# One attention-and-MLP kernel: a new written-out order of all steps, and twelve more products of ones

## Chip, cores and metric

The kernel runs on one core of one Trainium2 chip. The metric is the device time of one execution in microseconds (us). TensorE does the matrix products, VectorE (DVE), ScalarE (ACT) and GpSimd (POOL) the elementwise work, and SyncE (SP) issues nearly all DMAs; the stores are issued by ScalarE.

## The reference

An attention layer with two fixed sparsity patterns (heads 0 to 3 see the last 32 positions, heads 4 to 7 the earlier positions of the same residue modulo 32) is followed by an MLP whose hidden layer is a SoLU with layer norm.

```python
# q, k, v: 8 batches x 8 heads x 576 positions x 64
scores = scale * np.matmul(q, k.transpose(0, 1, 3, 2))
scores = np.where(masks[None, :, :, :], scores, -1000000000.0)
scores = scores - np.max(scores, axis=-1, keepdims=True)
attn = np.exp(scores)
attn = attn / (np.sum(attn, axis=-1, keepdims=True) + 1e-09)
x = np.matmul(attn, v)          # then (8 * 576) x 512
h = x @ w_in                    # 512 x 1024
e = np.exp(h - np.max(h, axis=-1, keepdims=True))
solu = h * (e / (np.sum(e, axis=-1, keepdims=True) + 1e-09))
mu, var = np.mean(solu, -1), np.mean((solu - mu) ** 2, -1)
out = ((solu - mu) / np.sqrt(var + 1e-06) * g_ln) @ w_out   # 1024 x 512
```

## The kernel before

The program is a list of steps. Each step is put on the list by `add(engine, cost, function, r=..., w=...)`, where `r` and `w` name what it reads and writes; a step is one to a hundred instructions of one engine. The list is not issued in the order in which it is written down: `ORDER`, a string of step numbers, gives the order of issue, and each engine works off its own steps in that order, waiting for what a step depends on. The costs do not enter the program; they served a search outside of it that wrote `ORDER`.

The attention of batch b is cut into four units, U(4b) to U(4b+3): two of strided heads and two of local heads. A unit's scores are one step of TensorE (U5>s, line 469), its maxima, differences and sums are steps of VectorE (lines 476 to 504), its exponentials of ScalarE, and its product with v is one step of TensorE (U5>x, line 561), whose two halves ScalarE and VectorE bring to SBUF as two float16 parts (lines 582, 583). From batch 1 on the probabilities are turned by a DMA transpose.

The tokens are cut into 36 tiles of 128, F0 to F35. A tile's first product is two steps of 12 matrix products each (lines 625 to 627: high by high, high by low, low by high, over four chunks of 128), and its second product is two more (lines 695 to 697). Between them stand the softmax-like factor and the layer norm on VectorE, ScalarE and GpSimd, and a DMA transpose.

Before F0 can run, w_in (four loads of 1 MB of 64-bit values, w0 to w3) has to be decoded (ScalarE line 734, GpSimd line 739, VectorE line 740), scaled by a sum of squares that needs all four, and split into two float16 parts (ScalarE line 761, VectorE line 762). w_out goes the same way (o0 to o3: decode, a Gram product on TensorE at line 777, a scale), but is needed only by the second products. Ahead of and between the first steps TensorE multiplies ones (line 248, `WARM` pairs), whose results nobody uses.

A SyncE step issues one DMA; SyncE takes its steps in the order of `ORDER` too, so a load that waits for its buffer holds back the loads and transposes behind it. Instructions themselves come to the engines as packets of DMA queues of their own (q8 and q14 on the page).

The last tile, F35, is stored in two halves: ScalarE scales and stores the left half, VectorE scales the right half into the same buffer `ob` and SyncE stores it.

Of the kernel before, what the change touches and what calls it, by code (L numbers as in the profile page):

```python
# [8 lines left out]
F16 = mybir.dt.float16  # L9
# [12 lines left out]
P = 128  # L22
# [40 lines left out]
105 87 54-55 59 45 88 36 62 46 106 89 107 47 108-109 39 90 120 80 121 91 144 64 137 48 63 145 49 110 136 146 92 122  # L63
163 147 123 79 60 65 81 61 66-67 29 68 124 69 286 16 138 17 125 18-19 148 139 162 95 149 126 82 140 83-84 96 93 70 94
141 165 97 287 85 164 168 142 111 150 41 77 42 113 151 290-291 166 100 112 98 73 40 114 78 178 101 99 292 75 127 115
74 129 128 293 152 170 173 153 116 130 155 117-119 131 71 306 156 180 307 167 76 132 134 72 294 179 135 169 133 322
288 308 175 206 295-296 181 476 154 208 174 171 309 207 310 209-210 329 213 311 323 176 157 160 312 211 214 297 345
330 477 172 158-159 298 331 177 212 313 346 182 226 324 183 299 314 300 348 215 228 325 347 184 161 332 289 216 349
227 217 350 333 315 229 354 246 230 334 327 231 185 301 304 218 355 220 335 232 186 336 305 302 356-357 233 303 187
337 480 248 316 234 249 247 194 235 250 317 221 328 320 318 481 321 266 188 251 190 326 358 338 252 536 482 195 339  # L70
236 483 237 253 192 238 200 222 496 268 319 189 240 340 204 193 191 359 513 202 497 219 360 223 267 343 196 341
361-362 254 344 371 535 363 198 498-499 519 512 269 645 270 255 271 520 484 256 241 538 272 257 201 197 273 203 373
199 537 521 224 258-259 522 539 364 342 239 274 644 225 143 540 275 372 485 374 205 276 486 370 544 351 260 277 375
261 376 392 378 365 500 545 377 242 278 393 487 368 243 280 681 394 379 478 380 281 383 366 523 546 244 369 395 262
547 396 279 479 488 397 648 245 398 413 399 649 489 415 514 367 414 650 400 404 651 416-417 680 490 282 515 703 516
664 263 548-549 264 524-525 541 491 517 381-382 384 418 420 401 386 501 387 665 421 502 492 503 494 402 652 434 419
542 403 436 504-505 834 385 425 405 265 422 666-667 687 435 506 455 526 437 493 518 407 283 423 438 406 352 527 441
456 550 653 551 495 704 528 424 439 507 388 688 408 706 508 284 510-511 529 440 835 457 689-690 442 705 707 668 509
446 530 708 285 654 552 712 691 531 669 458 443 459 462 553 533 692 709 426 713 460 670-671 428 389 534 554 646 429
390-391 532 463 870 714 560 444 715 409 543 445 716 581 655 838 447 871 430 647 461 449 693 555 464 717 561 582 839  # L80
694 656 467 427 562 465 657 672 695 353 840 556 841 558 673 563 410 557 658 836 448 710 564 567 565 411 450 566 466
572 568-569 559 583 674 659 854 412 584 570 842 682 855 602 468 451 843 431 728 893 696 585 697 683 662 432 571 586
470 588 573 660 894 575 471 661 593 587 589 433 603 576 590 856 663 604 623 857-858 686 844 605 1002 591-592 594 877
606 859 609 675 607 685 895 845 624 896 860 678 676 577 608 878 610 879-880 614 677 452-453 472 861 718 679 469 719
684 596 595 720 698 701 897 721 625 846 881 702 722 454 729 611 626 699 898 627 902 700 628 1003 597 723 630 903 629
574 631 862 612 904 632 905 882 635 731 598 730 863 613 732 906 1039 473-474 633 615 872-873 750 634 617 733-734 618
735 475 619 724 751 736-737 752 738 578 636 638 616 639 739 1006 753-754 757 755-756 758-761 883 762 741 771 899-900
726 847 837 579 1007 884 725 773 580 1038 740 727 1008 742 1009 744 848 901 745 774 885 792 1010 849 772 886 775 640
1022-1023 852 778 793 776 1004 599 1062 864 850 600 907 711 777 1024 779 746 874 780 763 1025 794 1061 851 783 765 887
766 853 637 1045 908 865 1046 601 1026 795 868 866 1047-1048 909 620 910 796 867 781 1005 797 875 798 743 876  # L90
1011-1012 621 813 815 869 911 622 641 799 1063 782 800 1049-1050 784 1251 1051-1052 804 1064 888 1065 801 642 814 816
802 786 912 817 891 818 787 892 889-890 1066 820 918 821 1086 1070 643 785 819 822 1192 919 803 920 767 921 913
823-824 1040 914 1071 922 1072 747 923 916 1073 748 825 805 925 788 1067 807 1041 764 1027 917 808 939 924 1013 915
941 1014 1028 1015 1029 926 749 768 940 942 1074 1042 1252 1016 1030 769 943 806 826 946 1053 944 828 809 1196 1075
829 1193 1054 770 927 1076 945 960 1077 928 1078 1043 962 1017 951 1194 929 1018 1229 1031 1197 789 961 1020 963 1032
947 964 1021 1019 930 790 967 827 1198 931 830 948 965 933 1033 949 1199 934 968 966 1212-1213 950 1200 791 983 810
1214 952 1055 954 1228 1215-1216 981 1360 1201 1217 1253 969 1235 984 955 1254 1044 1036-1037 1034-1035 982 1056 972
1236 985 1059 935 986 811 970 812 1237 971 1202 1361 1060 987 1238 1087 1255 1089 988 1218-1219 1088 1057 1256 1203
973 1257 1079 989 975 1260 953 990 1090 991 1239 993 1091 1094 1240 831 1362 832 1058 1220 1080 1241 976 1081 833 1230
1261-1263 1231 1221 1082 1108 936 1397 937 1095 1364 932 1195 1109 1092 956 1093 1110 1129 1242 1111-1112 1232 1084  # L100
1096 992 1068 938 957 1204 994 1097 1099 958 1085 996 1205 1115 1363 1206 997 1113-1114 1116 1131 1083 1130 977 974
1117 1098 959 1100 1120 1102 998 1118 1150 1103 1132-1133 1207 1119 1121 1208 1134 1222 1136 1151 1104 1365 978-979
1366-1367 1135 1209 1258 1123-1124 1210 980 1211 1264 1152 1380 1265-1266 1153 1243 1223 1137 1381 1233 1382 1368 1383
999 1154 1101 1125 1069 1267 1000 1157 1155-1156 995 1224 1138 1384 1171 1225 1396 1259 1435 1268 1234 1141 1158 1385
1139 1001 1386 1226 1244-1245 1140 1173 1172 1174 1122 1387 1159 1105 1269 1142 1144 1227 1175 1403 1246 1176 1143
1145 1369 1160 1247 1177 1106 1370 1161 1248-1250 1178 1371 1183 1179-1180 1278 1107 1270 1181 1388 1146 1182 1184
1186 1389 1276 1162 1277 1271 1279 1163 1372 1187 1165 1280 1166 1272 1373 1283 1281 1404 1126 1405 1398 1284 1127
# [54 lines left out]
def attn_solu_kernel(ctx: ExitStack, tc: tile.TileContext, qloc, qstr, kloc, kstr, vloc, vstr, w_in, w_out, g, masks, out):  # L162
# [637 lines left out]
    for b in range(B):  # L800
        if b:
            load_qk(b, 1)
        if b:
            v_split(b, 1)
# [86 lines left out]
```

## Time and profile before

| | |
|---|---|
| time before, median of 3 runs | 487.01 us (484.95 to 489.06) |
| the profiled execution's own time | 488.86 us |
| its span, first to last instruction | 487.1 us |
| TensorE busy | 470.0 us (96%), 6436 products |
| VectorE, ScalarE, GpSimd busy | 326.5, 336.3, 168.5 us |
| mean granted TensorE clock | 0.984 |
| moved by DMA | 83.87 MB, mean 172 GB/s |

The times stand against the span: 1.76 us of the profiled execution lie outside of it. "PE" is TensorE's products, "PEld" its weight loads, which are instructions of the same queue: each matrix product is one of either kind. A clock of 1.00 is 2.4 GHz, 0.50 is 1.2 GHz.

### The profile page before, as it was taken

What the parts mean: (1) busy time and instruction counts of PE and PEld (TensorE: products, weight loads), DVE (VectorE), ACT (ScalarE), POOL (GpSimd) and SP (SyncE); (2) the same over time, 40 slices, a digit from 0 to 9 for tenths busy, and PEclk for the clock granted to TensorE, in tenths of its full rate; (3) what the DMA queues carried; (4) which work ended last, traced back from release to release, by engine and by line L of the source; (5) the groups of instructions that cost most, each with busy time, mean ns of one, the idle gap of its engine ahead of it and who ended that gap; (6) DMA issues with size and microseconds to landing.
All of it is one profiled execution on the core that took longest, in us unless ns stands there. A gap on an engine that the chain in (4) does not pass through costs nothing.

```text
span 487.1 us, 15063 instructions
## 1 busy us (share of the span) xinstructions
PE 470.0 (96%) x6436; PEld 244.0 (50%) x6436; DVE 326.5 (67%) x698; ACT 336.3 (69%) x555; POOL 168.5 (35%) x328
## 2 busy tenths in 40 slices
PE   8867989999999999999999999999999999999996
PEld 3645655555555555455454555545545544444442
DVE  0889799898788776777758666776656474444430
ACT  2498699798878878867675885855776565565450
POOL 5465425452623432242152314331234242232220
PEclk9995998999999999999999999999999999999999
DMA  8998689678979996657996992678573786405332
GB/s 331 419 372 321 182 189 261 141 163 228 183 186 201 209 222 125 175 78 166 268 163 138 250 220 72 109 155 157 128 132 62 137 148 115 87 23 129 74 84 81
DMA packets 131763, 83.87 MB, mean 172 GB/s; under 512 B 117424, under 2 KB 118288, under 8 KB 131184
## 3 DMA queue, kind: packets, MB, share of 16 engines
q1 hardware_dynamic: 126512, 73.60, 65.5%
q10 hardware_dynamic: 5184, 9.31, 5.6%
q8 instruction: 50, 0.82, 0.7%
q14 instruction: 17, 0.14, 0.1%
HBM read 39.90 MB, written 9.44 MB: 101 GB/s over the span
## 4 chain that ended last, share of the span: by engine, by line
PE 87%; DVE 5%; DMA 5%; issue 1%; SPq 0%; ACT 0%; ACTq 0%
PE o_ps L695 12%; PE h_ps L625 12%; PE h_ps L626 12%; PE o_ps L697 12%; PE h_ps L627 12%; PE o_ps L696 12%; PE s_ps L469 6%; PE x_ps L561 5%; DMA vrs<-vstr 3%; DMA q<-qstr 2%; DVE w L762 1%; DVE obuf L740 1%; DVE m L476 0%; DVE m L499 0%; DVE st L631 0%
## 5 line engine op out<-in xcount | busy, mean ns | idle before, releaser
L695 PE MATMUL o_ps<-ohi,cc 128*128 128x512 f16 x272 | 103.3, 380 | 0.0
L697 PE MATMUL o_ps<-ohi,cc 128*128 128x512 f16 x272 | 103.1, 379 | 0.0
L696 PE MATMUL o_ps<-obuf,cc 128*128 128x512 f16 x272 | 103.1, 379 | 0.0
L631 DVE TENSOR_REDUCE st<-h_ps 128x1 f32<-128x512 f32 x70 | 47.3, 684 | 42.6 <-PE h_ps L627 40.5
L507 POOL TENSOR_TENSOR t<-t,m 128x540 f32<-128x540 f32 (+5 forms) x32 | 42.7, 1339 | 87.9 <-DVE m L504 74.0
L683 DVE SCALAR_TENSOR_TENSOR cc<-raw,st,cc 128x1024 f16<-128x1024 f32 (+1 forms) x38 | 46.6, 1232 | 30.1 <-ACT cc L682 30.0
L635 ACT ACTIVATE raw<-h_ps,st,vsc 128x512 f32<-128x512 f32 x62 | 47.9, 775 | 23.5 <-DVE st L633 22.5
L626 PE MATMUL h_ps<-w,xl 128*128 128x512 f16 x140 | 54.0, 386 | 1.8 <-DVE obuf L740 1.8
L637 DVE SCALAR_TENSOR_TENSOR raw<-h_ps,raw 128x512 f32<-128x512 f32 x70 | 47.0, 682 | 12.2 <-ACT raw L635 11.4
L625 PE MATMUL h_ps<-w,xl 128*128 128x512 f16 x140 | 54.2, 387 | 0.3 <-DVE raw L637 0.3
L682 ACT ACTIVATE cc<-raw,st 128x1024 f16<-128x1024 f32 (+1 forms) x38 | 41.6, 1100 | 18.3 <-POOL st L672 17.3
L627 PE MATMUL h_ps<-w,xl 128*128 128x512 f16 x140 | 54.1, 386 | 0.0
L625 PE MATMUL h_ps<-w,xs 128*128 128x512 f16 x140 | 53.6, 383 | 0.0
L626 PE MATMUL h_ps<-w,xs 128*128 128x512 f16 x140 | 53.5, 382 | 0.0
L627 PE MATMUL h_ps<-w,xs 128*128 128x512 f16 x140 | 53.1, 379 | 0.0
L641 ACT ACTIVATE raw<-raw,st 128x1024 f32<-128x1024 f32 x36 | 41.2, 1144 | 16.7 <-DVE st L640 13.8
L697 PEld LDWEIGHTS <-cc 128*128 128x128 f16 x288 | 28.1, 98 | 34.0
L703 ACT ACTIVATE ob<-o_ps,st 128x512 f32<-128x512 f32 x34 | 23.2, 683 | 31.7 <-PE o_ps L697 25.9
L695 PEld LDWEIGHTS <-cc 128*128 128x128 f16 x288 | 28.1, 98 | 33.0
L696 PEld LDWEIGHTS <-cc 128*128 128x128 f16 x288 | 28.2, 98 | 32.1
L670 POOL TENSOR_SCALAR st<-st 128x1 f32<-128x1 f32 x32 | 8.8, 275 | 88.7 <-ACT raw L642 88.0
L642 ACT ACTIVATE raw<-raw 128x1024 f32<-128x1024 f32 x36 | 37.9, 1054 | 2.2 <-ACT ob L703 1.7
(187 smaller groups left out, 841.1 us busy)
## 6 DMA issues: line engine op xcount, KB each, us to landing
out<-ob ACTq DMA_DIRECT2D x35, 256.0 KB, 3.5
k<-kstr SPq DMA_DIRECT2D x8, 594.0 KB, 5.2
q<-qstr SPq DMA_DIRECT2D x8, 594.0 KB, 5.9
k<-kloc SPq DMA_DIRECT2D x8, 576.0 KB, 5.7
q<-qloc SPq DMA_DIRECT2D x8, 576.0 KB, 6.4
raw<-w_in SPq DMA_DIRECT2D x4, 1024.0 KB, 6.8
ve<-vl SPq DMA_DIRECT2D x7, 480.0 KB, 4.0
vrs<-vstr SPq DMA_DIRECT2D x4, 768.0 KB, 6.3
```

The costliest lines, as they stand in the source:

```text
L507: add("pool", nx * nk / 520 + 0.03, lambda: nc.gpsimd.tensor_tensor(t4, t4, sm2.unsqueeze(3).broadcast_to([P, 2, nb, nk]), op=ALU.mult), r ...
L625: nc.tensor.matmul(hv[i], xhi[cc], whi[:, cc, cols], start=(cc == 0), stop=False)
L626: nc.tensor.matmul(hv[i], xhi[cc], wlo[:, cc, cols], start=False, stop=False)
L627: nc.tensor.matmul(hv[i], xlo[cc], whi[:, cc, cols], start=False, stop=(cc == 3))
L631: add("dve", 0.69, lambda i=i: nc.vector.tensor_reduce((nm, nm2)[i], hv[i], axis=AX.X, op=ALU.max, negate=True), r=[HH[i]], w=[(ST, "nm", i)])
L635: add("act", 0.73, lambda i=i, q=q: nc.scalar.activation(e[:, parts2[i]], hv[i], AF.Exp, bias=nm, scale=hs, accum_out=q), r=[HH[i], (ST, " ...
L637: add("dve", 0.7, lambda i=i, x=x: nc.vector.scalar_tensor_tensor(u[:, parts2[i]], hv[i], 1.0, e[:, parts2[i]], op0=ALU.mult, op1=ALU.mult ...
L682: add("act", w / 1200 + 0.295, lambda cols=cols: nc.scalar.mul(c[:, 0, cols], u[:, cols], r), r=[(U, 0), (U, 1), (ST, "r")], w=CC[0][mine])
L683: add("dve", w / 980 + 0.23, lambda cols=cols: nc.vector.scalar_tensor_tensor(c[:, 1, cols], u[:, cols], r, c[:, 0, cols], op0=ALU.mult, o ...
L695: nc.tensor.matmul(o, ct[:, cc, :], ohi[:, cc, :], start=(cc == 0), stop=False)
L696: nc.tensor.matmul(o, ct[:, cc, :], olo[:, cc, :], start=False, stop=False)
L697: nc.tensor.matmul(o, ct[:, 8 + cc, :], ohi[:, cc, :], start=False, stop=(cc == 7))
```

## The change

1. `ORDER` is replaced as a whole: all 1553 steps stand in a new order, found by a search on a replay of the program in which the fetches of instructions wait behind the transfers that are under way.
2. `LATE = 6` adds six steps of TensorE, each two products of ones with 480 columns, which write the bank `h_ps[1]` and nothing else. They are put on the list behind U3 of batch 0; `ORDER` places them among the attention of batch 0.
3. The right half of the last tile goes through the other `ob` buffer.
4. A memset of 8 columns becomes one of 32; an estimated cost changes from 0.62 to 0.7.
5. New paths for a sum of squares on TensorE (`V_PE`) and for split scores (`QF`) are written, and both sets of batches are empty, so none of their steps is put on the list.

```diff
+LATE = 6
+V_PE = ()
+QF = ()
...
 ORDER = """
-0-1 27 2 30 24 22 50 3-10 51 56 52 31 28 23 35 11 32-34 25 43 20 12 26 13 57 38 14-15 102 44 37 103-104 58 86 53 21
...
+1 3-5 39 31 28 6-9 22 2 34-35 20 44 32 27 23 33 10 46 29 56 11 79 30 86 102 45 87 103 25 88 104-105 38 12 58 57 13 106
...
-    add("dve", 0.1, lambda: nc.vector.memset(s_ps[:, 1, 504:512], 0.0), w=[("s", 1)])
+    add("dve", 0.1, lambda: nc.vector.memset(s_ps[:, 1, 480:512], 0.0), w=[("s", 1)])
...
-            add("dve", 0.42, lambda: nc.vector.tensor_scalar(ob[:, ends[1]], o[:, ends[1]], f, None, op0=ALU.mult), r=[O, (ST, "f"), OB], w=[(*OB, 1)])
-            add("sp", 0.4, lambda: nc.sync.dma_start(out[n * P : (n + 1) * P, ends[1]], ob[:, ends[1]]), r=[(*OB, 1)], w=[(*OB, 2)])
+            ob2, OB2 = ob_sb[(n + 1) % 2], ("ob", (n + 1) % 2)
+            add("dve", 0.42, lambda: nc.vector.tensor_scalar(ob2[:, ends[1]], o[:, ends[1]], f, None, op0=ALU.mult), r=[O, (ST, "f")], w=[OB2, (*OB2, "m")])
+            add("sp", 0.4, lambda: nc.sync.dma_start(out[n * P : (n + 1) * P, ends[1]], ob2[:, ends[1]]), r=[OB2], w=[(*OB2, 2)])
...
-            add("act", 0.62, lambda cc=cc: nc.scalar.mul(ohi[:, cc], obuf[:, cc], gs_sb[:, cc : cc + 1]), r=["gs", ("od", cc)], w=[("oh", cc)])
+            add("act", 0.7, lambda cc=cc: nc.scalar.mul(ohi[:, cc], obuf[:, cc], gs_sb[:, cc : cc + 1]), r=["gs", ("od", cc)], w=[("oh", cc)])
...
         if b == 0:
+            for i in range(LATE):
+                add("pe", 0.4, lambda: warm(2, [h_ps[1][:, 0:480]]), r=["ones"], w=[("h", 1)])
             prep_o()
```

Decoded, the two orders of TensorE from the scale of w_in to F3 are these, with the number of products in brackets ("ones" are pairs of products of ones, the new ones marked with a plus; U>t are transposes of batch 0's probabilities, o>g the Gram products of w_out, "scale" sums for a scale):

```
before: w scale(4) ones ones ones ones U0>t(3) scale(2) U0>t(3) U0>x(48) U1>t(3) U1>t(3) U4>s(48) U2>t(2)
  U1>x(40) U2>t(2) U3>t(3) U3>t(3) U2>x(48) U5>s(40) o0>g(8) F0(12) F0(12) U3>x(96) U6>s(80) o1>g(8) o2>g(8)
  o3>g(8) F1(12) F1(12) o scale(2) scale(2) F2(12) U4>x(72) U7>s(64) F2(12) U5>x(60) U8>s(48) F3(12) F3(12)
after: w2>g(8) w3>g(8) U0>t(3) scale(2) U1>t(3) ones+ w scale(4) ones+ ones+ U0>x(48) U2>t(2) U4>s(48) ones+
  U1>t(3) U2>t(2) U1>x(40) U3>t(3) U5>s(40) o0>g(8) U3>t(3) o1>g(8) U2>x(48) ones+ o2>g(8) o3>g(8) U3>x(96)
  o scale(2) U6>s(80) F0(12) F0(12) scale(2) F1(12) U7>s(64) F1(12) U4>x(72) U8>s(48) F2(12) F2(12) U5>x(60) ... F3(12) F3(12)
```

The sixth new pair stands ahead of the stretch shown, behind the Gram product of w1. On VectorE the last split of w_in (w0, line 762) is its 46th step before and its 58th after; ahead of it come now, in addition, the decodes of o1, o2 and o3, the maximum, difference and sum of U5, the sum of U4 and the Gram sum of w_out, while the sums of U2 and U3 stand earlier than before. On SyncE the first load is v of batch 0's local heads (640 KB), which came after all of w_in before, and the order of w_in's chunks is w0, w2, w1, w3 instead of w1, w2, w0, w3. The loads of v of batch 2 follow those of q and k (local heads, batch 1) and precede k and q (strided heads) of batch 2; those of v of batch 3 stand before and behind the transpose of U5's probabilities, where they stood behind it. From F3 on the two orders of TensorE differ in which halves of tiles lie between which units; the work is the same.

## Rows read from the trace of the kernel before

**Rows 1.** Busy times by stretch: us, busy (instructions) by engine, granted clock, DMA share, GB/s
```profile
0.00:84.00 84.00, 70.76 (x1317) 43.65 (x1318) 63.73 (x138) 61.09 (x98) 40.98 (x58) 0.92 0.89 297
84.00:483.20 399.20, 399.20 (x5121) 200.32 (x5119) 262.30 (x559) 274.71 (x457) 127.47 (x270) 1.00 0.69 147
```

**Rows 2.** Timeline of TensorE around the first token tile: start, us, what, [idle before <-releaser]
```profile
43.30 0.63 PE L625 MATMUL h_ps<-w,xl 128*128 128x512 f16 x1
45.77 0.59 PE L626 MATMUL h_ps<-w,xl 128*128 128x512 f16 x1 [1.84 <-DVE obuf L740]
...
48.88 0.38 PE L625 MATMUL h_ps<-w,xs 128*128 128x512 f16 x1
...
51.90 0.38 PE L627 MATMUL h_ps<-w,xs 128*128 128x512 f16 x1
```

**Rows 3.** Timeline of TensorE around the second stop
```profile
68.73 0.72 PE L561 MATMUL x_ps<-pt,vs 54*64 54x54 f16 x58
...
69.30 1.24 PE L469 MATMUL s_ps<-k,q 64*54 64x54 f32 x39
72.12 0.43 PE L469 MATMUL s_ps<-k,q 64*54 64x54 f32 x8 [1.59 <-issue]
```

**Rows 4.** Granted clock (after the engines) of two stretches, columns of rows 1
```profile
38.38:48.62 10.24, 7.52 (x106) 4.83 (x105) 9.72 (x14) 8.39 (x12) 5.71 (x4) 0.50 0.87 332
...
72.51:75.92 3.41, 3.41 (x13) 1.20 (x10) 3.41 (x7) 3.38 (x7) 0.00 (x0) 0.50 0.92 121
```

**Rows 5.** Instructions of TensorE (PE and PEld) by stretch
```profile
0.00:36.40 36.40, 27.81 (x474) 18.01 (x477) 20.58 (x56) 20.96 (x30) 19.12 (x37) 1.00 0.97 375
0.00:45.70 45.70, 34.37 (x603) 23.19 (x604) 29.68 (x70) 29.19 (x43) 23.41 (x40) 0.92 0.98 371
45.70:72.10 26.40, 24.51 (x511) 14.17 (x510) 22.80 (x48) 20.77 (x37) 11.24 (x9) 0.94 0.71 188
```

**Rows 6.** Part 3 of the page: packets, MB, share of the instruction queue
```profile
q8 instruction: 50, 0.82, 0.7%
```

**Rows 7.** DMA queues from 36.4 to 43.2 us: the only one with packets
```profile
q1 hardware_dynamic: 620, 2.44, 102.0%
```

**Rows 8.** DMA queues from 43.2 to 44.4 us
```profile
q8 instruction: 1, 0.02, 5.7%
```

**Rows 9.** DMA queues from 69.8 to 70.9 us
```profile
q8 instruction: 1, 0.02, 5.5%
```

**Rows 10.** Timeline of all engines at the end
```profile
483.32 0.47 ACT L710 ACTIVATE ob<-h_ps,st 128x256 f32<-128x256 f32 x1 [4.54 <-PE h_ps L697]
...
483.83 0.48 DVE L714 TENSOR_SCALAR ob<-h_ps,st 128x256 f32<-128x256 f32 x1 [11.00 <-ACT ob L710]
```

**Rows 11.** Timeline of TensorE: steps that move ahead of the first token tile
```profile
52.21 0.32 PE L561 MATMUL x_ps<-pt,vl 64*64 64x32 f32 x8
...
53.52 0.30 PE L561 MATMUL x_ps<-pt,ve 64*64 64x32 f32 x8
53.74 1.14 PE L469 MATMUL s_ps<-k,q 64*32 64x64 f32 x80
54.82 1.55 PE L777 MATMUL o_ps<-obuf 128*128 128x128 bf16 x24
```

**Rows 12.** Timeline of VectorE from the last decode of w_in on
```profile
23.81 1.22 DVE L740 SCALAR_TENSOR_TENSOR cc<-cc,raw 128x1024 int32<-128x1024 int32 x1 [1.38 <-POOL raw L739]
...
30.25 0.94 DVE L486 TENSOR_REDUCE m<-t 128x12 f32<-128x768 f32 x1
...
41.92 0.62 DVE L583 TENSOR_TENSOR xl<-x_ps,xl 128x256 f16<-128x256 f32 x2
42.60 0.72 DVE L476 TENSOR_REDUCE m<-s_ps 128x10 f32<-128x540 f32 x1
...
47.59 0.70 DVE L496 TENSOR_TENSOR t<-s_ps,m 128x540 f32<-128x540 f32 x1
...
53.24 0.71 DVE L499 TENSOR_REDUCE m<-t 128x10 f32<-128x540 f32 x1
```

More of the change, by code (lines that the diff above doesn't have):

```diff
@@ L66 @@
[L66 to L70, printed above, removed]
@@ L224, in attn_solu_kernel @@
     olo = obuf.bitcast(F16).rearrange("p c (a f) -> p c a f", a=2)[:, :, 0, :]
+    kf = obuf.bitcast(F16).rearrange("p (i j c) (a f) -> p i j c a f", i=2, j=2, a=2)[:, :, :, :, 1, :]
+    qf = more[:, VW[0] + VW[1] :].bitcast(F16)
+    NB2 = SP // QS
     whi, wlo = w16[:, :, 0, :], w16[:, :, 1, :]
@@ L452, in unit @@
         by_pe = b == 0
+        split = half and b in QF
         if not by_pe:
-            add("act", nx * nk / 1200 + 0.17, lambda: nc.scalar.copy(sv, mk), r=[MK], w=SS)
+            if split:
+                add("act", nx * nk / 1200 + 0.17, lambda: nc.scalar.mul(sv, mk, qs_sb[b % 2][:, 5:6]), r=[MK, ("qs", b % 2)], w=SS)
+            else:
+                add("act", nx * nk / 1200 + 0.17, lambda: nc.scalar.copy(sv, mk), r=[MK], w=SS)
         heads = [(pair, h, slice(h * D, h * D + D), (h ^ pair) * D) for pair in range(2) for h in range(2)]
@@ L464, in qk @@
             for i in range(nb):
-                for a, w in parts:
+                for x, y in ((0, 0), (0, 1), (1, 0)) if split else ():
+                    for pair, h, hs, row in heads:
+                        q0, step = ((2 + pair) * SP + b0 + i, NB2) if x else (pair * NB2 + b0 + i, nqb)
+                        nc.tensor.matmul(sc_ps[pair][row : row + D, i * nk : (i + 1) * nk], qf[hs, q0 : q0 + (D - 1) * step + 1 : step],
+                                         kf[hs, y, j, pair, i * nk : (i + 1) * nk], start=False, stop=(i == nb - 1 and x == 1), skip_group_check=True)
+                for a, w in () if split else parts:
                     for pair, h, hs, row in heads:
@@ L721, in attn_solu_kernel @@
     ROOMS = [(raw_sb[:, 2 * i : 2 * i + 2], R) for i, R in enumerate((
-        [(("e", x), i) for x in range(2) for i in range(2)], [(("u", x), i) for x in range(2) for i in range(2)], [("room", 0), ("room", 1)], [("room", 2), ("room", 3)]))]
+        [(("e", x), i) for x in range(2) for i in range(2)], [(("u", x), i) for x in range(2) for i in range(2)], [("room", 0), ("room", 1)], [("room", 2), ("room", 3), ("roomq",)]))]
     LAST_ROOM = (cc_sb[:, 3:5].bitcast(I32), [*CT[1], *CT[2]])
@@ L800, in attn_solu_kernel @@
     for b in range(B):
-        if b:
+        if b and b not in QF:
             load_qk(b, 1)
+        if b in QF:
+            qk_split(b)
         if b:
@@ L816, in attn_solu_kernel @@
             v_scale(b + 1)
+            if b + 1 in QF:
+                load_qk(b + 1, 1)
+                qk_scale(b + 1)
             if b:
```

185 lines of the change are left out of this document (124 added, 61 removed).

## The prediction, made before the changed kernel ran

> **What bounds the kernel now.** I read the busy times by stretch first, because TensorE is busy for nearly the whole span and only the places where it isn't can give anything back. From 84.0 us to its last product TensorE is busy in every microsecond at full clock; the first 84 us hold 13.2 us of idle time and a mean clock of 0.92 [rows 1]. The products are the same after the change, so the time is their sum plus what is lost ahead of 84 us, plus the tail. Next the timeline of TensorE, for stops. There are two that no data explains. At 43.9 us the first token tile F0 stops behind its first product for 1.84 us; the profile puts this down to a decode of w_out, which F0 doesn't read [rows 2]. At 70.5 us U8's scores stop in their middle for 1.59 us with nothing to wait for [rows 3]. Then the granted clock: it is at half from 38.38 to 48.62 us, a stretch with 2.7 us of idle time, and again for the 3.41 us behind the second stop [rows 4].
>
> Last I count instructions. Products and weight loads up to the first stop are 603 + 604 = 1207, and from there to the second 511 + 510 = 1021 [rows 5]; the instruction queue q8 brings 50 packets and 0.82 MB, so 16 KB each [rows 6], and 12,872 instructions in 50 packets are 257 per packet. The stops lie four packets apart (1024, less a few instructions of the sequencer that aren't counted). Up to 36.4 us TensorE had used 951 instructions, exactly 256 fewer than at the first stop [rows 5]. So a block is entered at about 36.4 us; no instruction packet comes until 43.2 us, while the data queue fills the engines [rows 7]; one packet comes between 43.2 and 44.4 us [rows 8], and TensorE goes on 1.4 us later. Before the second stop a packet comes between 69.8 and 70.9 us [rows 9], 1.2 us ahead of the restart. I take it that the packet of the next block is asked for when a block is entered, lies behind the backlog of transfers (6.8 us the first time), and stops TensorE when the block is used up too soon.
>
> **The rule against it.** The rows show stops at multiples of a packet with a late packet ahead of each. The Trainium skill (Runtime: NRT & Kernel Launch, section "Instruction fetch mechanics") says that the sequencer fetches the next 16 KB block while it executes the present one, and that crossing a block costs little and is mostly hidden. The block of 256 agrees with the count; the hiding doesn't, at these two places of some fifty. By the rule alone the order could take no fetch stops away; that is among the rivals.
>
> **The tail.** VectorE's half of the last store begins at 483.83 us, when ScalarE's half ends (483.32 + 0.47), and is put down to it [rows 10]. With another buffer the halves run side by side: 0.5 us off the end. The buffer's earlier user, F34, is stored a few tiles' products before. Gain 0.5.
>
> **The start, up to F0.** Two things change. TensorE does more before F0: U3's product with v (52.21 to 53.74, 1.5 us), U6's scores (1.1) and three Gram products of w_out (1.55) move ahead of it [rows 11], 4.2 us of work that doesn't come later. And F0 comes later, because VectorE's last split of w_in does. Before, VectorE goes without a long gap from the last decode at 23.81 us to the residues that F0 needs, at 42.54 [rows 12]. Ahead of these come now the chain from 42.60 to 48.29 (U5's maximum and difference, U4's sum, two decodes of w_out; 5.7 us), U5's sum (0.71), and one more decode (1.22, as at 23.81); U3's sum (0.94) has moved ahead of the last decode [rows 12]. So F0 at 42.54 + 5.69 + 0.71 + 1.22 - 0.94 = 49.2 us. Before, F0's first nine products are done by 48.88 us and one more follows each 0.216 us ((51.90 - 48.88) / 14) [rows 2], so at 49.2 us it had done 9 x 0.216 + 0.32 = 2.3 us worth of full-clock work. The gain is 4.2 - 2.3 = 1.9 us.
>
> From this I subtract. By the counts in the listing and the offset of 1207, block ends lie now in U2's product with v (its 31st product), at the end of U3's product with v, in U7's scores (5th) and in U4's product with v (56th). The block between the first two holds only 1.5 + 0.4 us of U2 and U3 and two Gram products of 0.5 us, and its packet is asked for while v, k and q of batch 2 (2.6 MB) load. Without a backlog it comes in time; with a lag of 6.8 us it is some 5 us late. I take 1 us of delay for F0, nearer to the lower end because VectorE's chain holds TensorE there anyway. That leaves a gain of 0.9; range from -3.4 to 2.8 (last decode and F0 1 us earlier). That the load of v now comes first (640 KB at 371 GB/s, 1.8 us later for w3 [rows 5]) lies within it, as other decodes fill that time. The twelve new products are some 0.2 us each at full clock and mostly fill waits; I charge 0.4 us, between 0 and 2.4. They should keep the clock up through 38 to 48 us, which is in the 0.9 already, since F0's half-clock products are in the 2.3.
>
> **The second stop.** At 72.1 us the stop costs 1.59 us, and the 3.41 us at half clock behind it lose half of that, 1.70 [rows 3, 4]. The used-up block there held one token step (2.6 us), U5's product with v (0.7) and most of U8's scores (1.1) [rows 3]. In the new order that block falls apart: U8's scores stand with F2 around them. The gain is 3.3 us if nothing takes its place. The candidate is the block from U7's 5th to U4's 56th product: 0.9 us of scores, 2.6 of F1, 0.7 of U4, as short as the old one. It stops TensorE only if its packet lags by more than about 1.8 us, and the load of v of batch 3 (640 KB, 1.7 us) may lie just there. I take it as gone; bounds 0 and 3.3.
>
> **The rest costs nothing that the rows show.** From 84 us VectorE is busy 262 of 399 us and ScalarE 275 [rows 1], so an order that differs only in which halves lie between which units has cover; without it each hole would be idle time of TensorE in full. The wider memset and the new cost estimates change no work; the new paths put no step on the list. The loads of v of batch 3 wait for the split of batch 1's v, and U5's transpose stands behind one of them on SyncE; U5's product with v now comes two token steps later than U4's, 5 us that cover it.
>
> Sum: 0.9 + 3.3 + 0.5 - 0.4 = 4.3 us. The profiled execution took 488.86 us, 1.85 above the median of three; against its own time the forecast is 484.6, and against the median 487.0 - 4.3 = **482.7 us**.
>
> **Rivals.**
> 1. The stop moves to U4's product with v, clock loss and all: 487.0 - (0.9 + 0.5 - 0.4) = 486.0. For it: that block is as short as the one that stopped, and a load stands near. Against: at this point SyncE has issued less than before 70 us. Chance 0.27.
> 2. Slower: F0's block waits out the backlog. Its packet is asked for at about 44.2 us, lags 6.8, takes 1.1 to come and 1.4 to act: 53.5; then U6's scores, and F0 at 54.6. By then the old order has finished F0 (5.2 us) and 2.4 us more, so the start loses 7.6 - 4.2 = 3.4, and the idle time puts the clock at half again, 1.7. With the tail, and the second stop where it was: 487.0 + 3.4 + 1.7 - 0.5 = 491.6. It decides from a lag of about 1.5 us. Against it: the lag was 6.8 us only with w_out's loads queued, which are done by then. Chance 0.12.
> 3. The stops aren't fetches (the rule above): the new order takes away neither, and only start and tail count, 486.0 as in the first. The counts speak against it. Chance 0.04.
> 4. Everything falls early: F0 at 48.2, start 2.8, no stop, new products all hidden: 487.0 - 2.8 - 3.3 - 0.5 = 480.4. Chance 0.12.
>
> The forecast has 0.45. The range, 480.0 to 488.5, leaves out the far end of rival 2 and a little below rival 4. One per cent, 4.9 us, is about what a measurement of this kernel can tell from no change; below 482.1 lie rival 4 and the lower third of the forecast's spread, 0.30, and above 491.9 half of rival 2, 0.06.
>
> **What would show it.** In the changed profile TensorE's timeline should show F0 at 49 to 51 us with products of 0.22 us from the start, no idle piece over 1 us between F0 and 84 us, and no half clock around 72 us; the last two halves should start together. A stop in U4's product with v, 1021 or so instructions behind one in U2's, would show rival 1; a stop ahead of U6's scores, rival 2. Idle time of TensorE behind 84 us would make the forecast wrong in a way that no term here holds.

## The result and the profile after

The changed kernel took 494.17 us (492.50 to 495.47, 4 runs) against 487.28 us of the kernel before, measured beside it: 1.0147 times the time, with a 95% interval of 1.0105 to 1.019. It is 6.9 us slower. The forecast was 482.7 us and the range 480.0 to 488.5, so sign and range were both wrong. The profiled execution took 493.26 us; its span is 491.5 us.

Engines of the changed kernel (busy us, share of the span, instructions) and the granted clock in 40 slices:

```profile
PE 472.6 (96%) x6448; PEld 246.1 (50%) x6448; DVE 325.8 (66%) x698; ACT 335.9 (68%) x555; POOL 171.1 (35%) x328
...
PEclk9998899999999999999999999999999999999999
```

Twelve products more, and hardly any low clock. The same by stretch, in the columns of [rows 1]:

```profile
46.20:53.00 6.80, 5.52 (x110) 4.79 (x114) 4.90 (x11) 4.23 (x9) 1.52 (x2) 0.50 0.99 383
...
0.00:84.00 84.00, 71.23 (x1325) 45.08 (x1326) 65.45 (x144) 61.16 (x99) 36.25 (x56) 0.96 0.89 294
84.00:491.50 407.50, 401.36 (x5125) 201.06 (x5122) 260.39 (x555) 274.79 (x457) 134.90 (x273) 1.00 0.64 145
...
60.00:84.00 24.00, 24.00 (x489) 13.41 (x488) 22.76 (x53) 21.96 (x42) 9.42 (x14) 1.00 0.97 210
```

From 60 to 84 us TensorE is busy throughout at full clock: the second stop and the half clock behind it [rows 3, 4] are gone, as forecast. Behind 84 us, where nothing was idle before, 407.50 - 401.36 = 6.1 us are now idle; 4.0 of them are the tail, and 1.37 and 0.52 us are two stops that no data explains, at 142.1 and 364.4 us. TensorE's timeline shows what lies ahead of F0 (L644 is the product with v that was L561, L861 the Gram product, L549 the scores, L708 F0), and one place behind 84 us:

```profile
45.49 0.30 PE L644 MATMUL x_ps<-pt,vl 64*64 64x32 f32 x4 [1.28 <-DVE xs L666]
47.48 0.43 PE L644 MATMUL x_ps<-pt,ve 64*64 64x32 f32 x4 [1.68 <-DMA ve<-vloc]
...
49.12 0.98 PE L255 MATMUL h_ps<-ones 128*128 128x480 bf16 x2
49.90 1.92 PE L861 MATMUL o_ps<-obuf 128*128 128x128 bf16 x16
51.74 0.44 PE L644 MATMUL x_ps<-pt,vl 64*64 64x32 f32 x8
...
54.38 1.14 PE L549 MATMUL s_ps<-k,q 64*32 64x64 f32 x80
55.45 0.39 PE L708 MATMUL h_ps<-w,xl 128*128 128x512 f16 x1
...
139.50 0.93 PE L549 MATMUL s_ps<-k,q 64*32 64x64 f32 x64
140.36 0.39 PE L778 MATMUL o_ps<-ohi,cc 128*128 128x512 f16 x1
142.12 0.38 PE L779 MATMUL o_ps<-obuf,cc 128*128 128x512 f16 x1 [1.37 <-issue]
```

F0 starts at 55.45 us, without a stop in its middle [rows 2], but some 5 us later than forecast (49.2 and 1). U2's product with v waits for `ve`. This is a second copy of batch 0's v of the local heads, shifted by 32 positions; the first copy, `vl`, is the load that the section on the change names as the first, while the three loads of `ve` moved to the end of w_out's. A pair of ones and two Gram products (16 matrix products) follow at half clock, which is where 0.98 us for two products of ones comes from. SyncE's own timeline shows why `ve` is late:

```profile
29.06 6.52 SPq L353 DMA_DIRECT2D raw<-w_out  x2
36.43 0.37 SPq L353 DMA_DIRECT2D cc<-w_out  x1
36.85 1.39 SPq L353 DMA_DIRECT2D ve<-vloc  x3
```

The three loads stand behind all loads of w_out, two of which wait for their buffers. Before, they were issued at 25.49 us. The chain of waits of the changed kernel carries this load for 9.5 us:

```profile
37.81 9.53 DMA ve<-vloc
```

**What was lost where.** For each trace I took every product of TensorE except the ones, counted its piece at full clock whole and at half clock half, and subtracted the sum from the stretch. What is left is lost: waits, ones and low clock together, in whatever order the work stands.

```
trace              span   0-60   60-84   84-end   products
before            487.1   25.7     3.6      3.9      453.9
before, again     482.9   23.4     1.5      3.9      454.2
after             491.5   29.3     0.0      6.2      456.1
b_ve_late         488.5   29.8     1.5      3.9      453.4
b_shift12         487.4   23.2     1.4      8.0      454.7
b_late            488.7   25.9     1.2      6.7      455.0
b_late_w10        482.8   22.9     1.7      3.8      454.3
a_ve_early        490.0   29.3     0.2      6.1      454.4
a_no_late         490.7   31.0     0.8      4.8      454.1
a_ve_w10          489.9   31.0     0.0      5.6      453.4
a_f0_free2        500.2   30.9     4.1     10.3      455.1
```

Between the two profiled executions the start loses 3.6 us more, 60 to 84 us lose 3.6 less, and the rest 2.3 more; the products themselves took 2.2 us more, spread over all groups with none above 0.7, which I didn't pursue (over the traces of the table they range over 2.7 us). That makes 4.5 us, and the spans differ by 4.4. The two executions of the kernel before differ by 2.3 us in the start and by 2.1 us from 60 to 84 us, so a difference of that size between two single executions shows little; against the second one the changed kernel's start loses 5.9 us more.

### The profile page after: what moved, and what is told of

The parts are those of the page before. It is cut to its first block, busy times and chain, and to the rows that moved or that the text cites. A ratio compares the mean times of both kernels' runs of the same rounds, so it can differ in the third digit from the quotient of the medians.

```text
span 491.5 us, 15097 instructions
## 1 busy us (share of the span) xinstructions
PE 472.6 (96%) x6448; PEld 246.1 (50%) x6448; DVE 325.8 (66%) x698; ACT 335.9 (68%) x555; POOL 171.1 (35%) x328
## 4 chain that ended last, share of the span: by engine, by line
PE 87%; DMA 6%; DVE 2%; SPq 2%; issue 1%; POOL 0%; ACT 0%; DVEq 0%; ACTq 0%
PE h_ps L708 12%; PE h_ps L710 12%; PE h_ps L709 12%; PE o_ps L778 12%; PE o_ps L780 12%; PE o_ps L779 12%; PE x_ps L644 6%; PE s_ps L549 6%; DMA raw<-w_in 3%; DMA ve<-vloc 2%; SPq L353 1%; DMA ve<-vl 1%; SPq L769 1%; DVE m L586 1%; DVE cc L824 0%
## 5 line engine op out<-in xcount | busy, mean ns | idle before, releaser
L714 DVE TENSOR_REDUCE st<-h_ps 128x1 f32<-128x512 f32 x70 | 47.5, 683 | 65.2 <-PE h_ps L710 65.0
L590 POOL TENSOR_TENSOR t<-t,m 128x648 f32<-128x648 f32 (+5 forms) x32 | 39.8, 1247 | 59.4 <-DVE m L587 58.9
L708 PE MATMUL h_ps<-w,xl 128*128 128x512 f16 x140 | 53.2, 380 | 0.0
L708 PE MATMUL h_ps<-w,xs 128*128 128x512 f16 x140 | 53.1, 379 | 0.0
L710 PE MATMUL h_ps<-w,xl 128*128 128x512 f16 x140 | 53.1, 379 | 0.0
L709 PE MATMUL h_ps<-w,xl 128*128 128x512 f16 x140 | 53.1, 379 | 0.0
L780 PEld LDWEIGHTS <-cc 128*128 128x128 f16 x288 | 28.2, 98 | 36.4 <-issue 2.7
```

Source lines behind the costliest of these rows:

```text
L708: nc.tensor.matmul(hv[i], xhi[cc], whi[:, cc, cols], start=(cc == 0), stop=False)
L709: nc.tensor.matmul(hv[i], xhi[cc], wlo[:, cc, cols], start=False, stop=False)
L710: nc.tensor.matmul(hv[i], xlo[cc], whi[:, cc, cols], start=False, stop=(cc == 3))
L714: add("dve", 0.69, lambda i=i: nc.vector.tensor_reduce((nm, nm2)[i], hv[i], axis=AX.X, op=ALU.max, negate=True), r=[HH[i]], w=[(ST, "nm", i)])
L780: nc.tensor.matmul(o, ct[:, 8 + cc, :], ohi[:, cc, :], start=False, stop=(cc == 7))
```

## The experiments

Two accounts stood against each other for the start, and one for the rest. **The loads** (T1): `ve` behind w_out on SyncE delays U2's product and all behind it. **The queue**: whatever the loads do, F0 stands behind the whole chain of w_out and a later scale of w_in. **The block ends**: 24 instructions more on TensorE move every later end of a block of 256, so that other steps are cut. Orders are shown as the steps that move; a label that begins with b has the order of before, one with a that of after. Times are medians, ratios to the kernel before in the same session, with 95% intervals.

**b_again**, the kernel before once more.

> The kernel before, unchanged, for a second trace of it. If its losses are fixed by the program, the stops at 45.8 us (1.84) and 72.1 us (1.59) and both stretches at half clock come again, and the span is 487.1. If they vary from execution to execution, as the span of 487.1 near the top of its times suggests, a trace with a shorter span (484 to 485) has a shorter or no stop at one of the two places, and the 3.3 us that the forecast took from the second stop were not there in the median.

484.67 us, span 482.9. Its TensorE timeline, to be held against [rows 2, 3]:

```profile
43.99 0.63 PE L625 MATMUL h_ps<-w,xl 128*128 128x512 f16 x1
44.41 0.63 PE L626 MATMUL h_ps<-w,xl 128*128 128x512 f16 x1
...
66.90 1.24 PE L469 MATMUL s_ps<-k,q 64*54 64x54 f32 x39
69.22 0.43 PE L469 MATMUL s_ps<-k,q 64*54 64x54 f32 x8 [1.08 <-issue]
```

F0's stop isn't there; U8's is, behind the same 39 + 1 products, 1.08 us instead of 1.59, and no low clock follows. The same program lost 4.5 us less. U8's stop kept its place and lost a third of its length, F0's was gone, and the execution on which I had sized them was 2.4 us above the pooled median (486.41 us, 23 runs).

**b_shift12**, the kernel before with twelve products of ones with 8 columns in front: 24 instructions, no other change.

```diff
+        for i in range(12):
+            nc.tensor.matmul(o_ps[:, 0:8], ones, ones[:, 0:1].broadcast_to([P, 8]), start=True, stop=True)
```

> The kernel before with twelve products of ones with 8 columns at the front, where TensorE waits for the first loads: no work is added on the path, only 24 instructions ahead of all others, as many as the change adds. If stops sit at block ends, the stop in F0 moves 12 products earlier, into U5's scores or the Gram product of o0, the one in U8's scores moves from its 40th to its 28th product, and a stop of about 1.4 us comes in F4's or F5's second product near 141 us, as in the changed kernel; time 487 to 490. If stops belong to steps, they stay where they were and nothing comes at 141 us; time 485 to 487.5.

489.68 us, 1.0073 (1.0045 to 1.01): 3.5 us for twelve products of 8 columns. TensorE (L474 are U8's scores, L700 F4's second product):

```profile
66.86 1.03 PE L474 MATMUL s_ps<-k,q 64*54 64x54 f32 x27
68.96 0.83 PE L474 MATMUL s_ps<-k,q 64*54 64x54 f32 x20 [1.07 <-issue]
...
134.61 0.93 PE L474 MATMUL s_ps<-k,q 64*32 64x64 f32 x64
137.19 0.58 PE L700 MATMUL o_ps<-ohi,cc 128*128 128x512 f16 x1 [1.66 <-issue]
```

U8's stop has moved from behind the 40th product to behind the 28th, exactly the twelve products put in front. F0's stop, expected twelve products earlier as well, isn't there, as in b_again; in b_late, further on, it stands there with 0.29 us. And there is a new stop at 137 us with low clock behind it, the one that the changed kernel has at 142, besides one of 0.68 us at 95.2. The busy times of one block show why just there; counted back 256 instructions from the stop, it begins at about the 4270th product or weight load (the counts in these rows hold some 30 more, which were under way when the stretch began). Before, the block at this count runs from 137.59 to 141.58 us:

```profile
137.59:141.58 3.99, 3.99 (x149) 2.48 (x140) 3.79 (x12) 3.68 (x9) 0.37 (x1) 1.00 0.24 50
```

with the move, and in the changed kernel:

```profile
133.96:135.53 1.57, 1.57 (x150) 1.48 (x139) 1.57 (x6) 1.27 (x4) 0.00 (x0) 1.00 0.25 87
```

```profile
138.88:140.75 1.87, 1.87 (x147) 1.49 (x138) 0.32 (x2) 1.10 (x3) 0.00 (x0) 1.00 0.03 9
```

Moving the window by 24 instructions takes long products of F4 out of it and puts short products with v in. The block is used up in 1.57 and 1.87 us instead of 3.99. In the changed kernel the one instruction packet near it moves between 139.7 and 140.9 us, after the block was entered at 138.88, and TensorE goes on at 142.12:

```profile
q8 instruction: 1, 0.02, 5.3%
```

So the next block is there 3.2 us after the last was entered (3.2 in b_shift12 and 3.3 in b_late too), with the data queue nearly empty (DMA share 0.03). Here a block of 3.99 us passes and one of 1.87 doesn't, so backlog isn't needed for a stop. A short block alone doesn't make one either. The changed kernel uses up another block in 1.23 us, with no idle time at its end:

```profile
251.30:252.53 1.23, 1.23 (x129) 1.20 (x130) 0.33 (x2) 0.69 (x1) 0.00 (x0) 1.00 0.00 0
```

There the instruction packet had moved at 248.1 us, 3 us ahead of the block's first instruction and not 0.9 us behind it; a block of 1.44 us from 345.77 us, with its packet at 342.7, passes in the same way. What makes a packet early or late no run here shows.

**b_late**, the old order with the six new pairs of ones among batch 0's attention (24 instructions more), and **b_late_w10**, the same with six pairs of the front left out (equal count).

```diff
-        add("pe", 0.4, lambda: warm(2, [o_ps[:, 0:480]]), r=["ones"], w=["o"])
+        add("pe", 0.4, lambda i=i: warm(0 if i < 6 else 2, [o_ps[:, 0:480]]), r=["ones"], w=["o"])
```

> Order of before with the six new pairs of ones among the attention of batch 0 and nothing else, so 24 instructions of TensorE more than before; b_late_w10 had the same pairs at an equal count and measured 0.9964. Theory A (the count decides): all block ends lie 12 products earlier, a stop of 1 to 1.7 us on the first half of F4's second product near 137 us as in b_shift12, and a time of 487 to 489 us (1.001 to 1.006). Theory B (the pairs gain by themselves, the count is nothing): 484.5 to 486 us (0.996 to 0.999) and no stop at 137 us.

> The order of before with the six new pairs among the attention of batch 0, and without six of the first pairs: the new pairs alone, at equal instruction counts from U4 on. If they pay by holding the clock up: no half clock from 38 to 45 us, F0 no later than 45, time 483.5 to 485. If they stand in the way: 486 to 488.

b_late took 490.92 us, 1.0078 (1.0053 to 1.0104), and stops where it was expected to:

```profile
136.89 0.93 PE L549 MATMUL s_ps<-k,q 64*32 64x64 f32 x64
139.55 0.38 PE L778 MATMUL o_ps<-ohi,cc 128*128 128x512 f16 x1 [1.74 <-issue]
```

The time lies 2 us above the bound that I gave, and not all of the loss is this stop: the clock is at half from 42.15 to 48.98 us. b_late_w10 took 485.03 us, 0.9964 (0.9945 to 0.9983): the fastest kernel of the study, ahead of both. Its stretch from 36 to 48 us, and that of b_again:

```profile
36.00:48.00 12.00, 10.56 (x170) 6.80 (x171) 11.52 (x16) 10.95 (x17) 5.84 (x4) 1.00 0.97 339
```

```profile
36.00:48.00 12.00, 10.63 (x161) 7.30 (x162) 11.25 (x16) 10.36 (x17) 5.30 (x4) 0.72 0.98 339
```

TensorE is idle for about the same 1.4 us in both, but with ones spread among the waits the clock stays at 1.00 instead of 0.72 (3.4 us at half clock come earlier instead, from 13.25 us, where front pairs are missing). At an equal count the pairs keep the clock here, as the forecast had it. In b_late, with the same pairs, they don't: TensorE is idle for 2.2 us of this stretch, 0.69 of them in a wait for `ve`, and the clock averages 0.76. So its 24 instructions cost the stop at 139 us, 2.9 us more than in b_late_w10 with what else is lost behind 84 us; why its start loses 3.0 us more as well no run shows.

**b_late_w10_5**, the same kernel measured again, with 12 executions.

> b_late_w10 once more with more rounds: the old order with six of its pairs of ones moved from the front to batch 0's attention, at an equal count. If its gain is real, 484.2 to 485.6 us and a ratio with an interval below 1; if it was the chip's scatter, 1.000 within 0.002.

484.91 us, 0.9974 (0.9951 to 0.9997). The gain is real and small.

**b_warm10**, the kernel before without the six pairs of the front.

> The order of before without six of the first pairs of ones: 24 instructions fewer, block ends 12 products later everywhere. If block ends make the stops: the stop in U8's scores (1.1 to 1.6 us) moves into F3's fourth product, where the packet is there by then, and shrinks under 0.5 us; time 483.5 to 485.5, a little faster than before, unless a new short block meets a backlog further on (then 486 to 489 with one new stop at a block end).

486.79 us, 1.0000 (0.9982 to 1.0017). U8's stop went, and stops of 0.82 and 0.73 us came at other block ends, at 65.2 and 252.9 us (a wait of 0.66 us at 77.6 is for ScalarE's step on the scores): another position, another set of cuts, this time at no price, and without the gain that I expected.

**b_ones32**, the kernel before with the ones in float32, meant to move block ends without a change of order.

> The kernel before with the ones of its 22 pairs in float32: the pairs become longer per instruction or more instructions, which moves the block ends; the rest is the same. If stops sit at block ends, both known stops leave their places, by the number of instructions that the ones gain or lose, and the time moves by up to 3 us either way. If they belong to steps, they stay in F0 and U8.

523.30 us, 1.0774 (1.0724 to 1.0825). The time is some 37 us longer; by the accounting of the table the ones take 39 us instead of 10.6, and the start loses 45.9. The stops lie at other steps again, up to this one behind a Gram product:

```profile
83.66 1.44 PE L778 MATMUL o_ps<-obuf 128*128 128x128 bf16 x12 [3.32 <-issue]
```

The counts of instructions ahead of the four longest stops, modulo 256, are 181, 173, 169 and 161, close to those of other runs' stops in the same region (181 at U8's in the kernel before, 173 in b_shift12), so it speaks for the blocks; for a price it is of no use.

**b_ve_late**, the old order with the three loads of `ve` where the change has them. They bring v of batch 0, not of batch 2, as the expectation calls it.

```diff
 sp: load w_out chunk o1
-sp: load ve of batch 0 (3 DMAs)
 sp: load w_out chunk o3
 sp: load w_out chunk o2
+sp: load ve of batch 0 (3 DMAs)
```

> Order of before; only the three first loads of v of batch 2 are moved on SyncE behind the loads of the last two chunks of w_out, where the changed kernel has them. Theory A (these loads are what delays the start): U2's product with v, or the first units of batch 2, wait for them, the end of F3 goes from 74.8-79.3 us to 76.5-81, and the time rises by 1.5 to 4 us (ratio 1.003 to 1.008). Theory B (the late scale of w_in and the chain of w_out ahead of F0 in TensorE's queue do it, the loads alone don't): no wait over 0.5 us on these loads and a ratio of 0.998 to 1.002.

490.24 us, 1.0079 (1.0052 to 1.0107): 3.8 us for this one move. TensorE waits for the load, and the clock, at half from 37.32 us (38.38 before), stays there until 50.98 instead of 48.62 (45.00 in b_again):

```profile
46.10 0.43 PE L561 MATMUL x_ps<-pt,ve 64*64 64x32 f32 x4 [4.67 <-DMA ve<-vloc]
```

```profile
37.00:51.00 14.00, 8.87 (x148) 7.08 (x149) 8.79 (x16) 8.08 (x15) 2.82 (x3) 0.51 0.69 230
```

The start loses 29.8 us, as much as in the changed kernel.

**a_ve_early**, the reverse: the changed order with these loads ahead of o3 and o2 again.

> The changed order, with the three loads of v for the local heads (ve) put back ahead of the loads of o3 and o2 on SyncE; nothing else moves. Theory 1 (these loads gate U2's product with v, the wait drops the clock, and F0 comes at 55.4 us instead of 50): F0 at 50 to 52 us, no half clock between 46 and 53 us, time 489 to 491 against 494.2. Theory 2 (the late scale of w_in and the chains of VectorE and ScalarE behind it set F0, the loads only happen to land last): F0 at 53.5 us or later, time 492.5 to 494.

492.04 us, 1.0107 (1.0065 to 1.0148); 2.1 us below the changed kernel, which the intervals don't separate. F0 starts at 53.84 us instead of 50 to 52:

```profile
52.77 1.14 PE L549 MATMUL s_ps<-k,q 64*32 64x64 f32 x80
53.84 0.39 PE L708 MATMUL h_ps<-w,xl 128*128 128x512 f16 x1
```

No wait for `ve` is left, and the start still loses 29.3 us. T1 alone doesn't explain the changed order. But TensorE doesn't stand waiting for the chain of w_out either: from 43.56 us to F0 TensorE is busy nearly throughout, with a wait of 0.17 us for a decode of w_out, and at a clock of 0.61:

```profile
43.56:53.84 10.28, 10.11 (x263) 8.61 (x263) 8.58 (x16) 8.65 (x14) 3.80 (x4) 0.61 0.94 361
```

The clock was at half from 41.26 to 51.50 us, so the place of the wait is taken by slow work.

**a_recip**, a_ve_early with the small steps of VectorE for U2 and U3 behind w_in's last diagonal.

```diff
-dve: reciprocals of the sums of U2 and U3
 dve: decode w3, diagonal of w3
+dve: reciprocals of the sums of U2 and U3
```

> The kernel a_ve_early with the reciprocals of the sums of U2 and U3 moved on VectorE behind the diagonals of w_in's last chunk, so that the scale of w_in no longer stands behind steps that wait while GpSimd works. Theory A (the late scale delays F0): the scale's product comes 2 to 3 us earlier and F0 at about 51 us against 53.8, time 489 to 491 us. Theory B (F0 waits for the chain of w_out in TensorE's queue): F0 within 1 us of 53.8 and the time within 1 us of a_ve_early's 492.0.

495.71 us, 1.017 (1.0125 to 1.0215). The scale's product came 1.25 us earlier (31.50 against 32.75), not 2 to 3, and F0 at 55.38 with 17 us at half clock from 39.7. An earlier scale alone didn't bring F0 forward; what it would do at full clock stays open.

**a_f0_free** and **a_f0_free2** put F0 ahead of the decode and the Gram products of o2 and o3 (with the loads as in a_ve_early).

```diff
+pe: F0
 pe: Gram o2, Gram o3
-pe: F0
```

> The changed order with F0 cut loose from w_out: the three ve loads ahead of o3 and o2, w0's split ahead of the decodes of o3 and o2 on ScalarE and VectorE, and the Gram products of o2 and o3 with what hangs on them behind F0. If F0 came at 55.4 us because w_out's last loads and decodes stand ahead of it on three queues: F0 at 48 to 50.5 us and a time of 488 to 490. If the late scale of w_in alone sets it: F0 at 53 us or later and 491.5 to 493.

> The changed order, F0 cut loose from w_out as in the run before, with the queues behind it mended: w0's split, U2's residues and F0 stand ahead of the decode of o2, and U3's product with v, U6's scores and the Gram products of o2 and o3 behind F0. If w_out's place ahead of F0 cost the start: F0 at 48 to 50.5 us and 488.5 to 491. If w_in's late scale costs it: F0 at 52 us or later and 491.5 to 494.

The first failed as an edit: the split of w0 on VectorE stood ahead of the part of ScalarE that it needs, waited 3.14 us, and the time was 504.32 us, 1.0361 (1.032 to 1.0402). The second did what it should, and F0 starts at 48.53 us. Yet it took 498.78 us, 1.023 (1.0193 to 1.0268):

```profile
48.53 0.63 PE L708 MATMUL h_ps<-w,xl 128*128 128x512 f16 x1
...
60.17 0.19 PE L328 MATMUL s_ps<-vm,ones 128*128 128x1 bf16 x2 [2.60 <-ACT vs L398]
...
72.21 1.46 PE L549 MATMUL s_ps<-k,q 64*54 64x54 f32 x48 [1.79 <-ACT s_ps L529]
```

TensorE now waits for ScalarE's squares of v and its masks, which stand behind the moved work. F0 seven us earlier buys nothing by itself; what it overtakes is needed soon after. Of the 10.2 us by which its span exceeds that of a_ve_early, 3.9 are lost from 60 to 84 us and 4.2 behind 84 us, where 6.8 us are at half clock.

**a_no_late**, the changed order without the six new pairs (`LATE = 0`).

> The changed order without the six pairs of ones (LATE = 0). If they lie on the path to F0 (they are in-order work on TensorE, twice as long at half clock): 2.4 to 3.5 us less, 491 to 492. If they are hidden in waits: 494 within 1. If they hold the clock up, taking them away makes a longer stretch at half clock and 495 to 497.

492.73 us, 1.012 (1.0087 to 1.0153). The stop at 142 us is gone, and ahead of 60 us the clock is lower:

```profile
31.40:45.10 13.70, 10.34 (x198) 8.32 (x199) 11.72 (x26) 12.32 (x20) 3.95 (x4) 0.50 0.89 308
```

Without the pairs the start loses 31.0 us instead of 29.3, and the end 1.4 less. The first difference isn't beyond what two executions of one kernel show; the second is the stop (1.37 us). The two kernels' times aren't separated by their intervals.

**a_warm10** (the changed kernel without six front pairs, so the old count) and **a_ve_w10** (the same with the loads early: both suspects away).

> The changed kernel without six of the first pairs of ones, which lie in the wait for the first loads: as many instructions in all as before the change, and nothing else moved. If the late stops come from where the block ends lie: the stop at 142 us goes or moves to a place 12 products later, and with it 1.4 to 2.2 us of idle time behind 84 us; time 491.5 to 493. If not: the same idle time and 493.5 to 495.

> The changed kernel with both suspects taken away: the three loads of v ahead of the last two loads of w_out, as before, and six of the first pairs of ones left out, so that the count of instructions is that of before. Theory A (the two carry the loss, and add): 494.2 less 2.1 less 3.5 gives 488.6 us, between 487 and 489.5 (ratio 1.001 to 1.006), with U2's product not waiting for v. Theory B (the loss sits in the order as a whole, new waits take the place of the old ones, as in a_warm10): 490.5 to 492.5 us, with F0 at 53 us or later.

492.72 us, 1.0139 (1.0093 to 1.0185), and 491.62 us, 1.0108 (1.007 to 1.0147). In both the fetch stop at 142 us is gone. In a_warm10 a wait for data stands at a step before it, and the idle time behind 84 us is no less:

```profile
142.57 0.27 PE L644 MATMUL x_ps<-pt,ve 64*64 64x32 f16 x6 [2.42 <-DMA ve<-vl]
```

a_ve_w10 should have come to 488.6 us if the two costs added up. They don't: its start loses 31.0 us, and its F0 is at 54.33, behind 10.2 us at half clock from 41.40. The wait of a_warm10 belongs to the changed order itself: at the same product TensorE waits 0.26 us for this load in the changed kernel, 0.62 in a_no_late, 0.82 in a_ve_w10 and 1.42 in a_f0_free2 (not in a_ve_early and a_recip), and in none of the traces that have the old order there. So a second hole lies beside the fetch stop, and the one hides the other.

**a_then_b** and **b_then_a**, one order up to F3 and the other from there.

> The changed order up to F3's second half, the order of before for all steps that are left. Theories 1 and 2 (the loss lies ahead of F0): 491 to 493, no stop at 142 us. Theory 3: 487 to 489.

> The order of before up to F3's second half, the changed order for all steps that are left; no new ones, store of the last tile as changed. Theory 3 (the loss lies behind F3, in holes like the 1.37 us stop at 142 us): 489 to 491. Theories 1 and 2 (the loss lies ahead of F0): 486 to 487.5, the old start and half a microsecond off the tail.

a_then_b took 495.65 us, 1.0184 (1.0139 to 1.0229), above both forecasts: its start loses 30.0 us, as the changed kernel's, and the stretch behind 84 us 7.7. It also has the 24 instructions more, with fetch stops of 0.70 and 1.44 us at 101.7 and 143.8, and a wait of 0.97 at 90.4, so the old later part wins nothing back here. b_then_a took 492.64 us, 1.0117 (1.0079 to 1.0156), but its largest waits (1.76 us at 77.7, 1.21 at 80.8) stand at the seam, so its time tells nothing of the later part; its trace shows the wait for `ve` there once more, 1.38 us at 140.63.

## Why the prediction was wrong

**The step that failed is "The start, up to F0".** It gave a gain of 0.9 us, at worst a loss of 3.4; against the same profiled execution the start loses 3.6 us more, and against the second one 5.9. I had F0 at 49.2 us, by adding up VectorE's steps as if VectorE waited for nothing, and weighed only an instruction block against it. F0 came at 55.45, and three things stand behind it. First, I had read that the load of v of local heads comes first and priced it, but not that the same v's second copy, `ve`, moved on SyncE behind w_out's loads; these wait for buffers, and U2's product with v, ahead of F0 in TensorE's queue, waited for it. b_ve_late shows this move alone at 3.8 us. Second, I took the Gram products that move ahead of F0 as 1.55 us of work that only changes place. With them the Gram sum of w_out moves ahead of w_in's last split on VectorE, and it waits for TensorE's Gram product, which stands behind U2's product in TensorE's queue:

```profile
51.85 0.29 DVE L865 SCALAR_TENSOR_TENSOR diag<-o_ps,unit 128x128 bf16<-128x128 f32 x1 [0.60 <-PE o_ps L861]
...
52.69 1.28 DVE L846 SCALAR_TENSOR_TENSOR w<-cc,w_sc,w 128x1024 f16<-128x1024 f32 x1
```

So the split ended at 53.97 us, with TensorE's own delay in it; with `ve` early again it still ended at 53.05 and F0 came at 53.84. Third, nearly all of U2's and most of U3's product and the Gram products between them ran at half clock, from 46.2 to 53.0 us, where I had the ones keep the clock up. How much of the 3.6 us belongs to each in the changed order stays open: the causes cover each other, and taking one of them away there (a_ve_early, a_recip, a_f0_free2, a_ve_w10) left a start that loses 29 us or more, with 10 to 17 us at half clock.

**The second stop was right, and mis-sized for the median.** It is gone with its low clock, and 60 to 84 us lose 3.6 us less than in the execution I read, against 3.3 forecast. But b_again loses only 1.5 us there. The forecast subtracted the stop of an execution 1.85 us above its median (2.4 above the pooled one) from that median.

**Rivals.** The stop didn't move to U4's product (1), and F0's block didn't wait out the backlog (2): the idle time ahead of F0 is data, not fetch. At the block end that the prediction placed at the end of U3's product with v, and charged with 1 us, TensorE stopped for 0.11 us, and for 0.84 us in a_then_b. Rival 2 had the right sign, 491.6 us, and almost the right place of F0, 54.6 us, by another mechanism. Rival 3, that the stops aren't fetches, is refuted for U8's stop by b_shift12. (The chance of a time below 482.1 us adds up to 0.27 by the prediction's own shares, not to 0.30.)

**"The rest costs nothing" was wrong** by 2.3 us, and the prediction named the sign to look for: idle time behind 84 us. I had worked out block ends for the stretch ahead of 84 us only. The twelve ones are 24 instructions, each later end moves, and one lands so that a block of short products is used up in 1.87 us with its packet late. In the old order 24 instructions cost 3.5 us (b_shift12) and, with a longer half clock at the start, 3.8 us (b_late). The assumption that a packet is asked for when a block is entered holds at this place, and not at 251 us, where it moved 3 us earlier.

**The ones** were charged 0.4 us. In the trace they take 14.1 us instead of 10.6, 3.5 more, some of them at half clock; in a_no_late's one trace, without them, the start lost 1.7 us more and the end 1.4 less. Whether they pay for themselves in the changed order is not shown; in the old one, at an equal count, they gain (b_late_w10).

**The tail** gave nothing: 4.0 us instead of 3.9. With two buffers the halves should run side by side [rows 10]. They don't:

```profile
487.19 0.38 PE L780 MATMUL h_ps<-ohi,cc 128*128 128x512 f16 x1
487.78 0.48 DVE L798 TENSOR_SCALAR ob<-h_ps,st 128x256 f32<-128x256 f32 x1 [10.55 <-PE h_ps L780]
...
488.30 0.47 ACT L793 ACTIVATE ob<-h_ps,st 128x256 f32<-128x256 f32 x1 [5.18 <-DVE ob L798]
```

Now VectorE goes first and ScalarE follows 0.04 us behind its end. Both still read the same accumulator `h_ps`; that this is the reason was only argued, since no run gave them two. The buffer wasn't what ordered them.

## What to carry to other kernels

In a kernel that leaves no hole on its main engine, any instruction added to that engine, however short, moves every later fetch boundary: count how long each block lasts, over the whole program, and look for blocks that are used up faster than the next one arrives (here 1.87 us against 3.2). Such a block is a suspect, not a verdict: look in the trace for when its packet moves. When a step is moved, follow its inputs back to their loads and see what each load passes in its queue; its own duration is the smallest part of its price. And size a stop only after a second trace of the same kernel: here the same program lost 33.2 us in one and 28.8 in the other.

## What the runs showed of the hardware

VectorE's smallest steps took up to eight times as long beside GpSimd (1.44 us against 0.17). Three steps on 128x6 to 128x12 elements, VectorE's timeline of the changed kernel:

```profile
19.03 0.17 DVE L586 TENSOR_SCALAR m<-m 128x12 f32<-128x12 f32 x1
...
26.58 1.08 DVE L586 TENSOR_SCALAR m<-m 128x12 f32<-128x12 f32 x1
...
28.95 1.44 DVE L586 TENSOR_SCALAR m<-m 128x6 f32<-128x6 f32 x1
```

and GpSimd's:

```profile
26.54 1.09 POOL L590 TENSOR_TENSOR t<-t,m 128x540 f32<-128x540 f32 x1
28.07 2.29 POOL L590 TENSOR_TENSOR t<-t,m 128x768 f32<-128x768 f32 x1 [0.43 <-DVE m L587]
```

Each long one ends within 0.03 us of the GpSimd step beside it (27.66 against 27.63, 30.39 against 30.36); the first, with GpSimd idle, took 0.17 us. The Trainium skill (SBUF — State Buffer, section "Who interferes with whom") has VectorE, in modes that a TENSOR_SCALAR can enter, and GpSimd take turns on one port pair, the later one blocked for the whole instruction; these rows agree with it.

On the fetches, the Trainium skill (Runtime: NRT & Kernel Launch, section "Instruction fetch mechanics") holds that crossing a block is mostly hidden. That agrees at most of some fifty crossings here; at a few TensorE stopped for 0.5 to 1.9 us, in b_ones32 for up to 3.3, and 24 instructions decided at which. A block of 1.87 us stopped it when the packet moved 0.9 us behind the block's entry, one of 1.23 us didn't when it had moved 3 us ahead.

TensorE's clock held 1.00 over 12 us with ones among the waits and averaged 0.72 without them, with the same 1.4 us of idle time (b_late_w10 against b_again); with the ones and 2.2 us of idle time it averaged 0.76 (b_late).
